# RWKV-7 recurrence into a two-level MoE on one core: the next chunk's transpose ahead of the last one's, and heads placed by pair parity

## The chip, the cores and the metric

The kernel runs on one core of a Trainium2 chip. The metric is the device time of one execution in microseconds (us). TensorE (PE) does the matrix products, VectorE (DVE) and ScalarE (ACT) work on rows of 128 partitions, GpSimd (POOL) does elementwise work more slowly, and SyncE (SP) issues DMAs. Each engine takes its instructions in the order written in the program, apart from what semaphores make it wait for. PSUM has eight banks, into which TensorE writes.

## The reference

Everything is float32. First a recurrence per batch and head (4 batches, 8 heads, 768 steps, head size 40), then a mixture of experts on its output:

```python
for t in range(S):
    y[:, :, t] = np.einsum('bhd,bhde->bhe', rt, state)
    Sa = np.einsum('bhde,bhe->bhd', state, at)
    state = state * wt[:, :, None, :] - np.einsum('bhd,bhe->bhde', Sa, bt) \
            + np.einsum('bhd,bhe->bhde', vt, kt)
x = y.transpose(0, 2, 1, 3).reshape(3072, 320)
# per token: best of 4 groups (softmax of x @ w_group), best of its 4 experts,
# out = g_w * e_w * relu(x @ w1[g, e]) @ w2[g, e]
```

## The kernel before

The recurrence is done in 6 chunks (c) of 128 steps, each in two halves (c2) of 64. The 32 heads form two streams z of two batches each; a stream has 8 pairs i of heads, and j = 0, 1 is the head within a pair. `each()` runs over the 16 heads of a stream. A "half chunk" below is one pass q = 2c + c2 of the main loop, for both streams (c0 and c1).

For a chunk, all steps within a half are solved at once by a triangular inverse. `prep` makes the decay factors with two scans (`back`, `forth`) and multiplies them into `At` (`mul_a`) and the k and b keys (`mul_kb`). `products` (L426) makes the head's 64x64 products: the masked part `g` into G (VectorE, L433), the triangular part `t` into TT (ScalarE, L438, L439) and the transposed keys into KN (L453). Only the 32x32 diagonal blocks of the triangle are solved step by step: VectorE turns them (`solve_load`, L465), GpSimd masks and copies them (L469, L476) and takes 30 steps of two operations each (L486, L488); VectorE turns the result back twice (`turn_x`, L495, into X1; `turn_d`, L499, into DT). The off-diagonal block follows by two products, `merge_a` (L514, copied by L519) and `merge_b` (L528, copied by L531), with `move_d` (L505) moving a block in between; these are the joins. There are two of each per chunk, one for each half.

The chain of a half chunk and a stream is: `right` (L550 with G and v, L552 with At and the state, added in PSUM; copied to RHS by L554), `turn` (the state transposed, L559, into Sn), `ut` (L574, copied into VT by L577), `u` (L566, copied into VN), `update` of the state (L584, L586, and L589 at a chunk's end), `m` (L595, masked into MN by VectorE, L599), `y_state` (L605) and `y` (L612, scaled into R by L614). `finish` (L621) transposes y of the chunk before and makes the gate's logits; `finish_out` copies them (`xn`, L629) and reduces (L630).

The order is written by hand (the tile framework's manual schedule): each engine's queue is in the order of the calls in the loop over q. In the loop of chunk c, `products` and `prep` work for chunk c+2, so that GpSimd solves chunk c+1 or c+2 while the chain of c runs. PSUM's eight banks are three rings: four "nar" (products, m, finish), two "one" (ut, y_state, joins) and two "seq" (right, turn, u, update). After the last chunk comes the MoE, from 407 us on. Arrays lie with head j of a pair on partitions 64j to 64j+39.

## Time and profile before

| | |
|---|---|
| median of 3 runs | 705.15 us (704.52 to 708.0) |
| profiled execution | 709.33 us, span 707.6 us |
| PE matmul, busy | 601.4 us (85%), 11852 records |
| PE weight load | 513.3 us (73%) |
| DVE | 367.5 us (52%), 651 |
| ACT | 277.2 us (39%), 726 |
| POOL | 295.3 us (42%), 428 |
| granted clock, mean | 0.936 of full speed |

The profiled execution is one run; its span leaves out 1.73 us around it. Busy shares are means over two different parts: the recurrence until about 417 us, with all engines at work, and the MoE, with TensorE alone nearly full. A float32 matmul call shows as two records. "[0.53 <-X]" behind a row is the idle time of its engine just before it, and what ended it; "issue" there means that the profile shows nothing that was waited for. A time "t0" is the start of the first `right` of a half chunk.

### The profile page before, as it was taken

Reading aid. Unit: us, or ns where it says so; the run is one execution under the profiler, and the core shown is the slowest. Engines: PE = TensorE matmul, PEld = TensorE weight load, DVE = VectorE, ACT = ScalarE, POOL = GpSimd, SP = SyncE. Lnnn points to the kernel's source line nnn. Section 1 sums busy time; section 2 is a strip of 40 time slices with the busy share of each in tenths; the row PEclk is TensorE's granted clock in tenths of the full one; section 3 lists DMA queues with packets and bytes.
Section 4 is the critical chain, followed back from the end, with each engine's and each line's share of the span. In section 5 each row is a group of like instructions: output and inputs, shape, how many; then the busy total and the mean of one; then the engine's idle time right before and its main releaser. Section 6 shows DMA issues by size and latency. Waiting matters only on the chain. (4 is left out here: it accounts for less than half of the span.)

```text
span 707.6 us, 26969 instructions
## 1 busy us (share of the span) xinstructions
PE 601.4 (85%) x11852; PEld 513.3 (73%) x11852; DVE 367.5 (52%) x651; ACT 277.2 (39%) x726; POOL 295.3 (42%) x428
## 2 busy tenths in 40 slices
...
GB/s 141 121 114 1 94 27 111 59 69 151 96 86 138 94 47 154 42 185 91 29 50 224 34 58 132 173 251 178 181 183 191 190 194 192 181 177 203 89 13 15
DMA packets 128913, 84.19 MB, mean 119 GB/s; under 512 B 77897, under 2 KB 120967, under 8 KB 128788
## 3 DMA queue, kind: packets, MB, share of 16 engines
...
## 5 line engine op out<-in xcount | busy, mean ns | idle before, releaser
L486 POOL TENSOR_TENSOR tmp<-home,TT 128x30 f32<-128x30 f32 (+9 forms) x150 | 103.5, 690 | 11.4
L488 POOL TENSOR_TENSOR home<-home,tmp 128x30 f32<-128x30 f32 (+9 forms) x150 | 100.9, 672 | 11.8
L854 POOL DMA_INDIRECT out_dram<-homek,dst_v x28 | 27.7, 990 | 170.7 <-DVE homek L853 156.6
L426 PE MATMUL nar<-home,home 64*128 64x128 f32 x768 | 67.9, 317 | 31.5 <-DVE home L394 14.8
L426 PEld LDWEIGHTS nar<-home,home 64*128 64x128 f32 x768 | 58.6, 219 | 37.4 <-issue 20.9
L821 PE MATMUL nar<-homeg,home 128*128 128x192 f32 (+7 forms) x472 | 84.5, 333 | 1.2 <-DVE homeg L806 1.2
L821 PEld LDWEIGHTS nar<-homeg,home 128*128 128x128 f32 x472 | 76.9, 195 | 7.8 <-issue 4.7
L550 PE MATMUL seq<-VN,homeg 64*64 64x40 f32 x768 | 51.8, 238 | 14.5 <-ACT RHS L554 9.7
L438 ACT COPY TT<-nar 32x256 f32<-32x256 f32 x96 | 34.7, 362 | 71.3 <-PE nar L426 36.4
L550 PEld LDWEIGHTS seq<-VN,homeg 64*64 64x64 f32 x768 | 45.1, 143 | 17.4 <-ACT RHS L554 11.0
L552 PE MATMUL seq<-ST,home 64*64 64x40 f32 x768 | 51.1, 236 | 0.0
L599 DVE TENSOR_TENSOR MN<-nar,up 128x512 f32<-128x512 f32 x48 | 30.9, 686 | 37.4 <-PE nar L595 37.3
L842 PE MATMUL one<-home,homeq 128*128 128x320 f32 (+5 forms) x192 | 49.5, 436 | 0.0
L433 DVE TENSOR_TENSOR homeg<-nar,up 64x256 f32<-64x256 f32 x80 | 33.4, 418 | 23.9 <-ACT TT L439 16.0
L552 PEld LDWEIGHTS seq<-ST,home 64*64 64x64 f32 x768 | 45.2, 146 | 0.0
L469 POOL TENSOR_SCALAR_AFFINE_SELECT TT<-TT 128x1024 f32<-128x1024 f32 x6 | 8.3, 1379 | 83.1 <-DVE TT L465 83.1
L842 PEld LDWEIGHTS one<-home,homeq 128*128 128x128 f32 (+5 forms) x192 | 30.3, 172 | 16.1 <-issue 1.1
L842 PE MATMUL one<-home,DT 128*128 128x320 f32 (+4 forms) x160 | 40.6, 435 | 0.0
L831 ACT ACTIVATE homeq<-nar 128x384 f32<-128x384 f32 (+5 forms) x14 | 7.3, 524 | 80.9 <-PE nar L829 55.0
L792 POOL DMA_INDIRECT homeq<-x_nat,src_i x4 | 4.6, 1151 | 82.2 <-DVE pad L651 63.8
L853 DVE TENSOR_SCALAR homek<-one,homek 128x320 f32<-128x320 f32 (+4 forms) x15 | 8.2, 550 | 57.9 <-PE one L842 57.9
L595 PE MATMUL nar<-home 64*64 64x64 f32 x1536 | 31.7, 221 | 5.9 <-issue 5.7
...
## 6 DMA issues: line engine op xcount, KB each, us to landing
...
```

Of the source, the lines that this page charges most:

```text
L426: nc.tensor.matmul(ps[j][:, i, :], lhsT=KB[half(j), i0 + i, c2], rhs=At[half(j), 0:b + 1:b, :], start=True, stop=True)
L433: nc.vector.tensor_tensor(G[half(j), hs], ps[j][half(j), :, HW:], up2[half(j), None, :].broadcast_to([HW, NH, HW]), op=ALU.mult)
L438: nc.scalar.copy(out=TT[q:q + HB, ns], in_=ps[j][q:q + HB, :, HW:])
L486: eng.tensor_tensor(t3, W[:, r0:r2, s:s + 1].broadcast_to([P, m, n]), sub[:, s:s + 1, s + 1:].broadcast_to([P, m, n]), op=ALU.mult)
L488: eng.tensor_tensor(W[:, r0:r2, s + 1:], W[:, r0:r2, s + 1:], t3, op=ALU.subtract)
L550: nc.tensor.matmul(ps[half(1 - j), i, :], lhsT=self.G[half(j), i, :], rhs=self.VN[half(j), i, j, :], start=True, stop=False)
L552: nc.tensor.matmul(ps[half(1 - j), i, :], lhsT=self.At[half(j), 1 + 2 * i + self.c2, :], rhs=S0[half(j), i, :], start=False, stop=True)
L595: nc.tensor.matmul(ps[j][half(h), i, :], lhsT=self.VT[half(j), i, h, :], rhs=self.R[half(j), i, self.ts], start=True, stop=True)
L599: nc.vector.tensor_tensor(self.MN[:, j], ps[j], up2[:, None, :].broadcast_to([P, NI, HW]), op=ALU.mult)
L821: nc.tensor.matmul(ps[:, f, :], lhsT=w1s[:, ko, (g0 + f) * P:(g0 + f + 1) * P], rhs=xT[:, ko, :], start=(f == 0 and ko == 0), stop=False, ...
L842: nc.tensor.matmul(ps[half(k % 2, n)] if two else ps[:n], lhsT=hts[e % 2][:, f, h * P:h * P + n], rhs=wbuf[e % 3][2][:, f, :], start=(k < ...
L854: nc.gpsimd.indirect_dma_start(out=out[:, :], out_offset=bass.IndirectOffsetOnAxis(ap=part_of(dst_i, dst_v, n, h, e), axis=0), in_=yt[:n], ...
```

## The change

What the diff does:

- At, R, VT, VN and DT are laid out so that the head of a pair sits by parity. In At the two heads of a pair lie in different columns, each on its own 64 partitions, and the other 64 partitions of these columns take G (`g` writes there). VN holds v on one half and the state on the other (`put_state`, ScalarE copies after the states are updated). So `right` is one product of 128 rows where there were two of 64 added in PSUM.
- `mul_a` in one piece for 128 columns per head parity is `mul_at`; the mask `mask_g` works on 64 partitions at a time; `scale` is copied by ScalarE.
- R and VT hold even and odd pairs on different partitions (`load_two`), and `ut`, `m`, `y_state`, `y` use rows and columns accordingly; `ut` and `y_state` take both "one" banks.
- `turn` turns two heads with one product and writes a "one" bank.
- The joins are one product for two heads; results are copied in four quarters per join. X1 is gone, its place is the right part of the DT that is not in use.
- `solve_mask` writes W itself, and the copy is gone. `solve(c + 2)` stands ahead of `turn_x(c + 1)`. The guard sums W instead of the masked block, and later.
- In even half chunks, the four `finish` stand together ahead of both first joins, and the last joins follow; in odd ones both `right` and `turn` stand ahead of the products of the other chunk, one half of which moves behind `u`. `y_state` moves behind `update` and behind the second `products`, and the last half of `products` ahead of the last `y`.
- The tail's scratch tiles move from `homeg` to the end of `home1`; the guard's bound takes account of the diagonal.

```diff
+        def put_state(c, c2, z):
+            for j in range(2):
+                nc.scalar.copy(out=state["vn", c, c2, z][half(j), :, j, :], in_=ST[z][c2][half(j)])
+
...
-                nc.vector.tensor_copy(out=scale, in_=Rr[:, :, 1])
+                nc.scalar.copy(out=scale, in_=Rr[:, :, 1])
...
+            def mul_at():
+                for j in range(2):
+                    mine = At[half(j), 1:, :].rearrange("p (i k e) t -> p i k (e t)", k=2, e=2)[:, :, j, :]
+                    nc.vector.tensor_tensor(mine, mine, pq[half(j), :, :L], op=ALU.mult)
...
             def g(j):
+                o = half(1 - j)
+                dst = At[o, of_head(j, c2, i0, NH), :]
                 if raw:
...
         def mask_g(c, c2, z):
-            G = state["g", c, c2, z][0]
-            nc.vector.tensor_tensor(G, G, up2[:, None, :].broadcast_to([P, NI, HW]), op=ALU.mult)
+            for j in range(2):
+                o = half(1 - j)
+                mine = state["p", c, z][0][o, of_head(j, c2), :]
+                nc.vector.tensor_tensor(mine, mine, up2[o, None, :].broadcast_to([HW, NI, HW]), op=ALU.mult)
...
-        def solve_mask(c):
-            sub = state[c][:, :, :HB]
-            nc.gpsimd.affine_select(out=sub, in_=sub, compare_op=ALU.is_ge, fill=0.0, base=-1,
+        def solve_start(c, eng):
+            W, sub = ws[c % 2], state[c][:, 0]
+            state["W", c], state["sub", c] = W, sub
+            nc.gpsimd.affine_select(out=W, in_=sub, compare_op=ALU.is_ge, fill=0.0, base=-1,
                                     pattern=[[-1, HB], [1, HB]], channel_multiplier=0)
-            state["sub", c] = sub
-
...
         def guard(c):
-            nc.vector.tensor_reduce(out=t_sum[:, c, :], in_=state["sub", c], axis=AX.X, op=ALU.add,
+            nc.vector.tensor_reduce(out=t_sum[:, c, :], in_=state["W", c], axis=AX.X, op=ALU.add,
...
         def merge_a(c, c2):
-            TT = state[c]
-            ps = bank([P, NS, NI, HB], "one")
-            for z in range(NS):
-                for i, j in each():
-                    q, o = j * HW, j * HW + HB
-                    n = (c2 * NS + z) * NI + i
-                    nc.tensor.matmul(ps[o:o + HB, z, i, :], lhsT=TT[q:q + HB, n, HB:],
-                                     rhs=X1[q:q + HB, n, :], start=True, stop=True)
-            PX = X1[:, c2 * NS * NI:(c2 + 1) * NS * NI, :]
+            TT, X1 = state[c], x1(c)
+            n0, nn = c2 * NS * NI, NS * NI
+            ps = bank([P, nn // 2, HW], "one")
+            for k in range(nn // 2):
+                for j in range(2):
+                    rows, ns = half(j, HB), slice(n0 + 2 * k, n0 + 2 * k + 2)
+                    nc.tensor.matmul(ps[half(j), k, :], lhsT=TT[rows, 1, ns, :], rhs=X1[rows, ns, :], start=True, stop=True)
             for j in range(2):
                 o = j * HW + HB
-                nc.scalar.copy(out=PX[o:o + HB], in_=ps[o:o + HB].rearrange("p z i t -> p (z i) t"))
+                for e in range(2):
+                    nc.scalar.copy(out=TT[o:o + HB, 1, n0 + e:n0 + nn:2, :],
+                                   in_=ps[j * HW + e * HB:j * HW + (e + 1) * HB, :, e * HB:(e + 1) * HB])
...
             for j in range(2):
-                nc.scalar.copy(out=DT[half(j, HB), c2 * NS * NI:(c2 + 1) * NS * NI, HB:],
-                               in_=ps[half(j, HB)])
+                for e in range(2):
+                    nc.scalar.copy(out=DT[half(j, HB), n0 + e:n0 + nn:2, HB:],
+                                   in_=ps[j * HW + e * HB:j * HW + (e + 1) * HB, :, e * HB:(e + 1) * HB])
...
             def right(self):
-                S0 = self.S0
                 ps = bank([P, NI, D], "seq")
                 for i, j in each():
-                    nc.tensor.matmul(ps[half(1 - j), i, :], lhsT=self.G[half(j), i, :], rhs=self.VN[half(j), i, j, :],
-                                     start=True, stop=False)
-                    nc.tensor.matmul(ps[half(1 - j), i, :], lhsT=self.At[half(j), 1 + 2 * i + self.c2, :],
-                                     rhs=S0[half(j), i, :], start=False, stop=True)
+                    nc.tensor.matmul(ps[half(j), i, :], lhsT=self.At[:, 1 + 4 * i + 2 * j + self.c2, :],
+                                     rhs=self.VN[:, i, j, :], start=True, stop=True)
                 nc.scalar.copy(out=self.RHS, in_=ps)
 
             def turn(self):
-                ps = bank([P, NI, D], "seq")
-                for i, j in each():
-                    nc.tensor.matmul(ps[half(j, D), i, :], lhsT=self.S0[half(j), i, :], rhs=eye[half(j), :D],
+                ps = bank([P, NI, D], "one")
+                for i in range(NI):
+                    i0 = i - i % 2
+                    nc.tensor.matmul(ps[half(i % 2, D), i0:i0 + 2, :], lhsT=self.S0[:, i, :], rhs=wsel[:, 0, :2 * D],
                                      start=True, stop=True)
                 nc.scalar.copy(out=self.Sn[:, :, :D], in_=ps)
...
             def ut(self):
-                ps = bank([P, NI, HW], "one")
+                ps = [bank([P, NI // 2, HW], "one") for _ in range(2)]
                 for i, j in each():
-                    nc.tensor.matmul(ps[half(j, D), i, :], lhsT=self.RHS[half(1 - j), i, :],
-                                     rhs=self.DT[half(1 - j), self.un * NI + i, :], start=True, stop=True)
+                    nc.tensor.matmul(ps[j][half(i % 2, D), i // 2, :], lhsT=self.RHS[half(j), i, :],
+                                     rhs=self.DT[half(j), self.un * NI + i, :], start=True, stop=True)
                 for j in range(2):
-                    nc.scalar.copy(out=self.VT[half(j), :, 1 - j, :], in_=ps[half(j)])
+                    nc.scalar.copy(out=self.VT[:, j::2, 1, :], in_=ps[j])
...
                 for i, j in each():
+                    k, n = i % 2, i - i % 2 + j
                     for h in range(2):
-                        nc.tensor.matmul(ps[j][half(h), i, :], lhsT=self.VT[half(j), i, h, :],
-                                         rhs=self.R[half(j), i, self.ts], start=True, stop=True)
+                        nc.tensor.matmul(ps[k][half(1 - j if h == 0 else j), n, :], lhsT=self.VT[half(k), n, h, :],
+                                         rhs=self.R[half(k), n, self.ts], start=True, stop=True)
...
             def y_state(self):
-                self.ps_y = bank([P, NI, HW], "one")
+                self.ps_y = [bank([P, NI // 2, HW], "one") for _ in range(2)]
...
+                for k in range(2):
+                    nc.vector.tensor_tensor(self.R[:, k::2, self.ts], self.ps_y[k], self.pq[:, k::2, self.ts], op=ALU.mult)
...
+        ALL2 = (("back",), ("mul_kb", 0), ("forth",), ("mul_at",), ("mul_kb", 1))
...
-                pre(("back",))
+                finish(c - 1, 1, 0)
+                finish(c - 1, 1, 1)
+                merge_a(c, 0)
                 merge_a(c, 1)
-                move_d(c, 1)
-                if q == 2 * NC - 4:
-                    choose(0, N3, fl, rl, (1,))
-                finish(c - 1, 1, 0)
-                merge_b(c, 0)
-                finish(c - 1, 1, 1)
                 finish_out(c - 1, 1, 0)
                 finish_out(c - 1, 1, 1)
                 load_r(c, 1)
-                merge_b(c, 1)
+                pre(("back",))
+                if q == 2 * NC - 4:
+                    choose(0, N3, fl, rl, (1,))
+                for c2_ in range(2):
+                    move_d(c, c2_)
+                    merge_b(c, c2_)
                 if q == 2 * NC - 4:
                     rank_products(0, N3)
                     ranks(0, N3)
                     seen_by(N3)
-                pre(("forth",), ("mul_kb", 0), ("mul_a", 0))
+                pre(("forth",), ("mul_kb", 0), ("mul_at",))
...
+                c0.right()
+                if q >= 2 * NC - 3:
+                    choose(*new_gate[q], fl, rl, (0,))
+                c0.turn()
+                if new:
+                    load_at(*new)
+                pre(("back",))
+                c1.right()
+                c1.turn()
+                if old:
+                    products(*old, 1, 0)
+                pre(("forth",))
                 if q >= 2 * NC - 3:
                     choose(*new_gate[q], fl, rl, (1,))
-                pre(("mul_kb", 0), ("mul_a", 0))
             c0.ut()
             c0.u()
+            if c2:
+                if old:
+                    products(*old, 1, 1)
+                pre(("mul_kb", 0), ("mul_at",))
...
-            c0.y_state()
             c0.m()
             c0.update()
+            c0.y_state()
...
                     load_vn(*nxt, z)
+                for z in range(NS):
+                    put_state(*nxt, z)
...
-            c1.y_state()
             c1.m()
             if nxt:
                 for z in range(NS):
                     load_vt(*nxt, z)
-            if q:
-                pre(("mul_a", 1))
             if new:
                 products(*new, 0, 1)
+            c1.y_state()
...
+            kn1 = products(*new, 1, 1, late=True) if kn else None
             c1.y()
             if kn is not None:
                 kn()
+                kn1()
                 pre(("squares", 0))
             if q == 0:
                 pre(("mul_kb", 1), ("mul_a", 1))
-                guard(1)
-            elif c2 == 0 and c + 1 < NC:
-                guard(c + 1)
-            if c2 and new:
-                products(*new, 1, 1)
-            if c2 and c + 1 < NC:
+            if c2 == 0:
+                guard(c)
+            elif c + 1 < NC:
+                if new:
+                    solve(c + 2, PO)
                 turn_x(c + 1)
-                if new:
-                    solve_load(c + 2)
-                    solve_mask(c + 2)
-                    solve_start(c + 2, PO)
-                    solve_steps(c + 2, PO, 0, HB)
                 turn_d(c + 1)
```

ScalarE's queue in an even half chunk (chunk 2), from the copies behind the first `right` on; `one_109` and `one_110` are the two "one" banks, `home_116` is VT, `DT` the inverse. Before:

```order
L519 COPY X_134<-one_109 32x512 x2
L505 COPY DT_121<-DT_121 32x16x32 x2
L629 COPY xn<-nar_105 128x320
L629 COPY xn<-nar_106 128x320
L519 COPY X_134<-one_110 32x512 x2
L505 COPY DT_121<-DT_121 32x16x32 x2
L531 COPY DT_121<-one_109 32x16x32 x2
L629 COPY xn<-nar_107 128x320
L629 COPY xn<-nar_108 128x320
L531 COPY DT_121<-one_110 32x16x32 x2
L577 COPY home_116<-one_109 64x8x64 x2
```

Now:

```order
L651 COPY xn<-nar_106 128x320
L539 COPY TT<-one_109 32x8x32 x4
L539 COPY TT<-one_110 32x8x32 x4
L651 COPY xn<-nar_107 128x320
L651 COPY xn<-nar_108 128x320
L526 COPY DT_120<-DT_120 32x16x32 x2
L553 COPY DT_120<-one_109 32x8x32 x4
L526 COPY DT_120<-DT_120 32x16x32 x2
L553 COPY DT_120<-one_110 32x8x32 x4
L406 COPY scale<-Rr 128x8
L597 COPY home_116<-one_109 128x4x64
L597 COPY home_116<-one_110 128x4x64
```

The copies of the two first joins (L539) now stand together behind the first two `xn` (one is shown), all four `xn` stand ahead of the moves (L526), and `ut`'s copies (L597) take both banks.

VectorE's queue in an odd half chunk, from the `back` scan to MN of the first stream; `homeg` is G, `home_115` At of the chunk ahead, `nar` the banks of `products` and of `m`. Before:

```order
L383 SCALAR_TENSOR_TENSOR Rr<-home_114,first 128x1040
L385 RECIPROCAL first<-Rr 128x8
L433 TENSOR_TENSOR homeg<-nar_105,up_132 64x256
L433 TENSOR_TENSOR homeg<-nar_106,up_132 64x256
L388 SCALAR_TENSOR_TENSOR homeq<-home_114,first 128x1040
L390 COPY scale<-Rr 128x8
L433 TENSOR_TENSOR homeg<-nar_107,up_132 64x256
L433 TENSOR_TENSOR homeg<-nar_108,up_132 64x256
L398 TENSOR_TENSOR home_114<-home_114,Rr 128x8x128
L394 TENSOR_TENSOR home_115<-home_115,homeq 128x8x64
L599 TENSOR_TENSOR MN<-nar_105,up_132 128x512
```

Now, with MN (L620) next:

```order
L399 SCALAR_TENSOR_TENSOR Rr<-home_114,first 128x1040
L401 RECIPROCAL first<-Rr 128x8
L457 TENSOR_TENSOR home_116<-nar_105,up_131 64x4x64
L457 TENSOR_TENSOR home_116<-nar_106,up_131 64x4x64
L404 SCALAR_TENSOR_TENSOR homeq<-home_114,first 128x1040
L457 TENSOR_TENSOR home_116<-nar_107,up_131 64x4x64
L457 TENSOR_TENSOR home_116<-nar_108,up_131 64x4x64
L421 TENSOR_TENSOR home_114<-home_114,Rr 128x8x128
L417 TENSOR_TENSOR home_115<-home_115,homeq 64x8x128 x2
L620 TENSOR_TENSOR MN<-nar_105,up_131 128x512
```

The copy of `scale` has left the queue, and At's multiply is two pieces that cover both halves of the chunk; one multiply by the window (L421) stands ahead of it as before.

The end of VectorE's queue in an odd half chunk, where the solved blocks are turned. Before:

```order
L614 TENSOR_TENSOR home_116<-one_110,homeq 128x8x64
L433 TENSOR_TENSOR homeg<-nar_107,up_132 64x256
L433 TENSOR_TENSOR homeg<-nar_108,up_132 64x256
L495 STREAM_TRANSPOSE X_134<-home_115 128x32x32
L465 STREAM_TRANSPOSE TT<-TT 128x32x32
L499 STREAM_TRANSPOSE DT_121<-home_115 128x32x32
```

Now:

```order
L636 TENSOR_TENSOR home_116<-one_109,homeq 128x4x64
L636 TENSOR_TENSOR home_116<-one_110,homeq 128x4x64
L491 STREAM_TRANSPOSE TT<-TT 128x32x32
L516 STREAM_TRANSPOSE DT_121<-home_115 128x32x32
L520 STREAM_TRANSPOSE DT_120<-home_115 128x32x32
```

The turn of the next triangle (L491), on which GpSimd waits, now stands ahead of the turn of the solved one (L516), which waits for GpSimd; the last masks of `products` stand ahead of the last multiply of y.

## Rows read from the trace of the kernel before

**Rows 1.** Busy time by stretch: length, PE, PEld, DVE, ACT, POOL, clock, DMA share, GB/s.

```profile
92.87:144.29 51.42, 42.24 (x1384) 39.57 (x1376) 40.33 (x54) 32.09 (x88) 46.64 (x63) 0.93 0.28 61
137.89:197.20 59.31, 52.04 (x1730) 47.92 (x1729) 43.71 (x59) 37.15 (x99) 49.78 (x73) 0.97 0.44 103
197.20:227.83 30.63, 26.70 (x994) 24.56 (x992) 21.64 (x28) 19.85 (x47) 23.46 (x35) 1.00 0.45 111
227.83:252.34 24.51, 23.34 (x739) 21.60 (x737) 21.43 (x31) 16.57 (x50) 22.25 (x29) 1.00 0.40 85
252.34:308.20 55.86, 49.64 (x1731) 46.20 (x1729) 43.46 (x59) 36.74 (x97) 46.08 (x65) 1.00 0.40 96
...
407.00:707.60 300.60, 281.11 (x1758) 215.65 (x1750) 69.11 (x177) 33.57 (x107) 63.51 (x64) 0.98 0.47 153
146.59:150.00 3.41, 3.41 (x82) 3.35 (x76) 3.41 (x2) 1.16 (x2) 1.65 (x2) 0.50 0.02 5
```

**Rows 2.** GpSimd's line of time around the end of a solve.

```profile
253.44 0.27 POOL L488 TENSOR_TENSOR home<-home,tmp 128x30 f32<-128x30 f32 x1
258.64 1.27 POOL L469 TENSOR_SCALAR_AFFINE_SELECT TT<-TT 128x1024 f32<-128x1024 f32 x1 [4.94 <-DVE TT L465]
```

**Rows 3.** TensorE's line of time in the even half chunk from 197.20.

```profile
197.20 0.32 PE L550 MATMUL seq<-VN,homeg 64*64 64x40 f32 x4
...
198.74 0.31 PE L552 MATMUL seq<-ST,home 64*64 64x40 f32 x4
...
202.65 1.20 PE L514 MATMUL one<-X,TT 32*32 32x32 f32 x64
203.78 1.83 PE L621 MATMUL nar<-wsel,home 128*64 128x100 f32 x32
...
212.69 0.70 PE L574 MATMUL one<-DT,RHS 64*40 64x64 f32 x18 [1.42 <-issue]
...
217.06 0.27 PE L595 MATMUL nar<-home 64*64 64x64 f32 x1
217.10 0.23 PE L605 MATMUL one<-home,Sn 64*64 64x64 f32 x2
217.16 1.10 PE L595 MATMUL nar<-home 64*64 64x64 f32 x62
...
220.32 0.69 PE L584 MATMUL seq<-VN,homek 128*40 128x40 f32 x25 [1.17 <-issue]
220.81 1.10 PE L612 MATMUL one<-MN,homek 128*40 128x64 f32 x32
```

**Rows 4.** ScalarE's line of time in the same half chunk, the joins.

```profile
203.90 1.17 ACT L519 COPY X<-one 32x512 f32<-32x512 f32 x2 [0.70 <-PE one L514]
205.09 1.26 ACT L505 COPY DT<-DT 32x512 f32<-32x512 f32 x2
206.37 0.75 ACT L629 COPY xn<-nar 128x320 f32<-128x320 f32 x2
...
211.46 1.17 ACT L531 COPY DT<-one 32x512 f32<-32x512 f32 x2
```

**Rows 5.** VectorE's line of time in the odd half chunk from 227.83.

```profile
237.01 1.55 DVE L398 TENSOR_TENSOR home<-home,Rr 128x1024 f32<-128x1024 f32 x1
238.48 1.08 DVE L394 TENSOR_TENSOR home<-home,homeq 128x512 f32<-128x512 f32 x1
241.07 1.29 DVE L599 TENSOR_TENSOR MN<-nar,up 128x512 f32<-128x512 f32 x2 [1.51 <-PE nar L595]
...
254.58 1.95 DVE L495 STREAM_TRANSPOSE X<-home 128x1024 f32<-128x1024 f32 x1
```

**Rows 6.** Groups of instructions: count, busy us, mean ns, idle time before.

```profile
L438 ACT COPY TT<-nar 32x256 f32<-32x256 f32 x96 | 34.7, 362 | 71.3 <-PE nar L426 36.4 <-DVE homeg L433 14.4 <-POOL tmp L486 9.6
...
L461 DVE TENSOR_TENSOR homeg<-homeg,up 128x512 f32<-128x512 f32 x4 | 4.6, 1195 | 0.0
```

**Rows 7.** TensorE's line of time, the first join of the half chunk from 137.89.

```profile
146.26 1.72 PE L514 MATMUL one<-X,TT 32*32 32x32 f32 x64 [2.53 <-DVE X L495]
```

143 lines of the change are left out of this document (67 added, 76 removed).

## The prediction

> **What bounds the kernel now.** I read the table of stretches first [rows 1]. The tail from 407.00 on is 300.60 us with TensorE busy 281.11 of them; the diff moves two scratch tiles there and nothing else, so I take it as unchanged. All gain or loss lies in the first 407 us. A steady chunk of 128 tokens is an even and an odd half chunk, counted from the first product of `right` to the next one: 30.63 and 24.51. TensorE is busy 26.70 and 23.34 of them, VectorE 21.64 and 21.43, GpSimd 23.46 and 22.25. TensorE is nearest to full, so the plain reading is that it is the bound. The second view is GpSimd's line of time [rows 2]: the solve of one chunk ends at 253.71 and the next starts at 258.64, after 4.94 of waiting for VectorE's transpose. VectorE comes to the transpose that reads a solve's result at 254.58, without a wait [rows 5]. So GpSimd is not the bound either, though it is within a microsecond of being it, and its own work per chunk is 55.1 less that gap, 50.2, and less still by the copy that goes. The third view is TensorE's line of time through one even half chunk [rows 3]. Ahead of `ut` there is a gap of 1.42 that the profile calls issue; ScalarE's last join copy ends at 212.63, beside the end of that gap [rows 4]. In the odd half chunk VectorE waits 1.51 for `m` before MN at 241.07 [rows 5]. Three engines are close to each other, and each works in order.
>
> **TensorE's part.** `right` goes from 64 records of two quadrants to 32 over all 128 rows. The old groups of four take 1.54 for 52 records [rows 3], 29.6 ns each and 1.87 in all; `y`, which has the new shape, does 32 in 1.10. I take 1.03: 0.83 less per chain. `turn` goes from 32 records to 16 twice as wide: nothing. `ut` and `y_state` go from two quadrants to four: `m` does 62 records in four in 1.10, 18 ns each, so 32 take about 0.57 where at 29.6 they take 0.95: 0.37 less each. A join goes from 64 records in 1.20 to 32, about 0.93 by the same pace; with one first or last join per chain that is 0.27 at most, and I take 0.15. Sum 1.7 per chain, less what `m` may lose: its calls now stand four in a row on one row half, where the half changed after two. I put it at 1.35 instead of 1.10. Net 1.45 per chain, four chains per chunk: 5.8 of 50.0. If TensorE were alone, each chunk would gain that.
>
> The rows show that matmuls of neighbours do change places: a record of `m` starts at 217.06, ahead of records of `y_state` at 217.10, all of which stand before it in the order [rows 3]. The Trainium skill, page "TensorE: Matmul & The Clock Gate", Part 3 on packing small matmuls, has them in strict program order, with no reordering. The row speaks against it here; by that rule `m` would only ever pair two quadrants in the new order, which is rival C.
>
> **Even half chunk.** `right`, `turn`, `right`, `turn` now stand in a row (2 x 1.03 and 2 x 0.67: 3.4), then all four `finish` products (3.64, by 1.83 for two), then both first joins. The first one ends at t0+8.0, where it ended at t0+6.65 (202.65 and 1.20). From there ScalarE's queue is in order. A join's result is now copied in four quarters, as the two heads of a pair come from different places: 0.365 each by the row of the 32x256 copy [rows 6], 1.46 where two copies took 1.17 [rows 4]. So: four, four, two `xn` (0.75), two moves (1.26), four, two moves, four: 4 x 1.46 + 0.75 + 2 x 1.26 = 9.1, ending at t0+17.1. Before, `ut` of the first chain waited for the first bank of the joins alone. It now writes two banks, and the second is the one that the last join's copies empty. So `ut` starts at t0+17.2; it went on after its gap at t0+15.5. TensorE has nothing from t0+12 to t0+17.2. From 212.69 to the next half chunk it took 15.14; less 1.2 of an issue gap at 220.32, less 0.37 for two `ut` and two `y_state` each (1.48), 0.5 more for `m`, and 0.2 for the records ahead of 212.69, that is 13.2. Even half chunk: 17.2 + 13.2 = 30.4. Issue gaps may come back, 0 to 1.5; I take 0.7 and put it in the sum.
>
> **The clock.** After 2.53 without TensorE work before 146.26 the granted clock was 0.50 (1.2 GHz) from 146.59 to 150.00, and the join there took 1.72 where it takes 1.20 [rows 1, 7]. The hole of 5 us would do the same to `ut`, `u` and `m` behind it. Half of 3.4 us is 1.7 of work; I take 1.3 on the path, with bounds 0 and 1.7.
>
> **Odd half chunk.** VectorE has two scans, four masks, the multiply by the window (1.55) and one of At (1.08) ahead of MN, and without the wait it was ready at t0+11.7 [rows 5]. At now holds two heads apart, on 64 partitions each, and is multiplied as two pieces of 64x1024: between 2 x 1.08, the row of 512 elements, and 2 x 1.55, the row of 1024 beside GpSimd; 2.7 taken. VectorE is ready at t0+13.4. TensorE has `m` done at t0+10, since one half of `products` stands behind `ut` and `u` now; it waits, and its gain is lost in VectorE's queue. From MN on it took 11.3 to the next half chunk. The last `y` now stands behind the last half of `products`, whose banks come free only when VectorE's masks and ScalarE's copies of an earlier half are done: 0.8 more, 12.1. Sum 25.5, bounds 24.0 and 26.5.
>
> **What costs nothing here.** GpSimd's solve loses its copy and its gap, 6 us of GpSimd's time, and none of the end while the other engines need 55; the cover is theirs, and GpSimd is what is next when they shrink. The four copies of states into VN per half chunk fall into ScalarE's idle time, 30.63 less 19.85. Twelve more DMA issues per chunk stand on SP's queue with nothing that is waited for at once behind them. The guard reads W one half chunk later at the same cost.
>
> **Start.** Up to 144 VectorE carries most (40.33 of the last 51.42 [rows 1]). Added: eight-head masks, four of 64 partitions for two of 128, +2.4 by 1.195 each [rows 6], twice; and the multiply of At in four preparations, about +1.0 each. Part of this is covered by idle time, so of some 9 us I take 6 at t=137.9; bounds 3 and 9.
>
> **End.** In the last four half chunks the solves and then the products end, so TensorE carries a larger part still than the 23.34 of 24.51 of the odd half chunk [rows 1], and its saving counts. Even -1 and 0, as the copies' hole stays; odd -4.4 and -3.0, as there is no preparation ahead of MN and 2.9 to 3.2 of TensorE's work goes. -8.4.
>
> **Sum.** Start +6. Pairs of half chunks, even 30.4 + 1.3 and odd 25.5: 57.2 against 55.14 from 197.20 (+2.1) and 55.86 from 252.34 (+1.3) [rows 1]. The pair from 137.89 took 59.31, with the wait of 2.53; GpSimd starts earlier now, the wait goes, and I put it at 57.7 (-1.6). End -8.4. Returning issue gaps 4 x 0.7 = +2.8. Total +2.2: no change beyond what shows. The profiled run was 709.33 for a span of 707.60, so it would become 711.5; the median of the runs shown is 705.15, 4.2 below the profiled one, and the same difference on it gives **707**. This case's own range is 699 to 714.
>
> **Rivals.**
> *A, TensorE was the bound and the gain is paid out.* A chunk falls to GpSimd's 49.5 to 50: -6 for three chunks, -8.4 at the end, +6 at the start: 705 - 20 = 685. For it: TensorE's 23.34 of 24.51. Against: the queues of ScalarE and VectorE worked out above.
> *B, slower.* The holes of 2.6 in odd half chunks lower the clock too, as the 2.53 before 146.26 did: 1.3 more in each of five, with the start at +9 and the end at -6. That is 6.5 + 3 + 2.4 on top of the forecast, 719. It decides once TensorE's hole in odd half chunks is as long as that one.
> *C, matmuls keep their order.* `m` then costs 1.87 instead of 1.10, and not the 1.35 taken: 0.52 more in each of 24 chains, 18 of them on the path (in six the wait for VectorE hides it): +9.4, 716. This is what the rule of the Trainium skill named above would make of the change; that page stands alone against the row.
> *D, the solves don't close up,* as the last copies into TT hold back the transpose ahead of GpSimd. The forecast stays; A then stops at -10, 695.
>
> **Chances.** Forecast 0.50: of it faster 0.11, same 0.27, slower 0.12. A with its part of D 0.26, faster. B 0.16 and C 0.08, slower. Faster by over 0.5% 0.37, within 0.5% (3.5 us, about what a measurement of this kernel can tell from no change) 0.27, slower 0.36. The range goes from A to just short of B: 685 to 718.
>
> **What would show it.** Right: in even half chunks `ut` first at t0+17, with TensorE idle ahead of it and the granted clock lower behind it; in odd ones VectorE at MN without a wait, TensorE waiting for MN; GpSimd's solves at most 1 us apart and done well ahead of the transpose that reads them; the half chunk of 137.9 some 6 later. Wrong: chunks of 50 with GpSimd never idle and the transpose waiting for it (A); `m` in 1.9 (C); `ut` at t0+14 (the two banks then are not the wait).

## The result and the profile after

The changed kernel takes 713.73 us (median of 20 runs, 708.84 to 717.42); the kernel before takes 707.14 in the 20 runs made beside them. The ratio is 1.011, with an interval of 1.0087 to 1.0134: about 7 us slower. The forecast of 707 stood on a base of 705.15. The measured time lies in its range of 685 to 718, and just inside the narrower 699 to 714, but what was forecast was no change, and the change is a loss.

The traces compared are of one execution each: 709.33 us before (span 707.60) and 713.00 after (span 710.90). That is a difference of 3.3 in the spans, less than the 6.6 between the medians, because the profiled run of before was 2.2 above its median and that of after 0.7 below. What follows places the 3.3; where the rest lies in the other runs the two traces can't show.

The first lines of the page after: the span, then busy time, share of the span and records of each engine.

```profile
span 710.9 us, 23391 instructions
...
PE 581.1 (82%) x9932; PEld 491.8 (69%) x9932; DVE 384.0 (54%) x670; ACT 300.0 (42%) x836; POOL 299.7 (42%) x421
```

TensorE has 20 us less to do than before (601.4) in 1,920 records fewer. VectorE has 16.5 more and ScalarE 22.8 more. The mean granted clock fell from 0.936 to 0.889.

Busy time by stretch after, with the columns of [rows 1]. The first row ends where half chunk q = 2 starts, the next five are q = 2 and 3 together, 4, 5, and 6 and 7 together, then the last four half chunks, then the tail.

```profile
0.00:150.03 150.03, 83.34 (x1601) 75.44 (x1602) 122.64 (x181) 99.46 (x268) 63.79 (x109) 0.73 0.35 78
150.03:206.13 56.10, 46.74 (x1416) 43.29 (x1413) 45.88 (x61) 40.23 (x115) 46.86 (x63) 0.88 0.46 109
206.13:236.87 30.74, 25.37 (x775) 23.68 (x772) 23.77 (x29) 22.83 (x62) 25.05 (x35) 0.83 0.43 105
236.87:262.75 25.88, 21.66 (x647) 19.76 (x645) 22.00 (x31) 16.95 (x53) 21.79 (x28) 0.93 0.40 85
262.75:320.42 57.67, 47.33 (x1414) 43.69 (x1412) 45.64 (x60) 40.13 (x114) 46.78 (x62) 0.88 0.40 98
320.42:420.32 99.90, 83.40 (x2595) 77.45 (x2590) 60.60 (x149) 47.54 (x123) 32.26 (x63) 0.88 0.34 93
420.32:710.90 290.58, 273.22 (x1523) 208.54 (x1520) 63.51 (x163) 32.83 (x105) 63.19 (x64) 0.98 0.48 157
```

The same view of the kernel before, from q = 2 to the end of q = 7:

```profile
137.89:308.20 170.31, 151.72 (x5187) 140.27 (x5185) 130.24 (x175) 110.30 (x290) 141.57 (x201) 0.99 0.42 100
```

| stretch | before | after | difference | forecast |
|---|---|---|---|---|
| start, up to q = 2 | 137.89 | 150.03 | +12.14 | +6 |
| q = 2 to 7 | 170.31 | 170.39 | +0.1 | +1.8, and issue gaps +2.8 in all |
| q = 8 to 11 | 108.70 | 99.90 | -8.8 | -8.4 |
| tail | 290.70 | 290.58 | -0.1 | 0 |

So the steady part is where it was although TensorE's work there fell from 151.72 to about 141.1 (the four rows of after), the end pays out as forecast, and the start costs twice what was put on it.

**An even half chunk.** TensorE's line of time in the half chunk from 206.13 (start, busy, operation, records, and the idle time ahead with what ended it):

```profile
206.13 1.08 PE L571 MATMUL seq<-VN,home 128*64 128x40 f32 x32
...
209.06 2.92 PE L643 MATMUL nar<-wsel,home 128*64 128x100 f32 x64
211.91 2.08 PE L535 MATMUL one<-DT,TT 32*64 32x64 f32 x64
214.64 3.48 PE L549 MATMUL one<-DT,TT 32*64 32x64 f32 x64 [0.66 <-ACT TT L539]
219.58 0.43 PE L594 MATMUL one<-DT,RHS 64*40 64x64 f32 x2 [1.46 <-ACT DT L553]
222.38 0.98 PE L594 MATMUL one<-DT,RHS 64*40 64x64 f32 x27 [2.36 <-ACT DT L553]
```

`ut` (L594) starts at t0+13.46, with the first of its two banks, does two records and stops. The other 30 wait 2.36 us for the second bank and start at t0+16.25. Both waits name L553, the last joins' copies, which are the end of this queue on ScalarE:

```profile
213.10 3.00 ACT L539 COPY TT<-one 32x256 f32<-32x256 f32 x8 [2.02 <-PE one L535]
...
218.04 1.49 ACT L553 COPY DT<-one 32x256 f32<-32x256 f32 x4
...
220.84 1.49 ACT L553 COPY DT<-one 32x256 f32<-32x256 f32 x4
```

From 213.10 to 222.33 are 9.23 us without an idle stretch; the forecast added up 9.1 for the same queue, ending at t0+17.1 where it ended at t0+16.2.

**The clock.** Two stretches of the same half chunk (the granted clock stands third from the end of each row):

```profile
211.91:215.50 3.59, 2.94 (x94) 2.80 (x94) 1.16 (x3) 2.31 (x7) 2.96 (x9) 0.99 0.46 142
215.50:225.50 10.00, 6.04 (x136) 5.44 (x135) 8.73 (x8) 7.78 (x20) 9.45 (x8) 0.50 0.63 165
```

Of the two levels, 2.4 and 1.2 GHz, TensorE runs at the lower for 10 us. The fall comes at 215.50, while the last joins run. That is 0.9 after a hole of 0.66 ahead of these joins, and 2.6 before the first of the holes in front of `ut` opens, at 218.12. The same half chunk before was at 1.00 throughout [rows 1].

**An odd half chunk.** VectorE's line of time in the one that starts at 236.87:

```profile
246.61 3.15 DVE L417 TENSOR_TENSOR home<-home,homeq 64x1024 f32<-64x1024 f32 x2
249.79 1.29 DVE L620 TENSOR_TENSOR MN<-nar,up 128x512 f32<-128x512 f32 x2
```

VectorE comes to MN (L620) at t0+12.9 without a wait, and the wait of 1.51 in [rows 5] is gone: `m` had been done since t0+9.7.

### The profile page after: what moved, and what is told of

It is laid out like the page before. It is cut to its first block, busy times and chain, and to the rows that moved or that the text cites. A ratio compares the mean times of both kernels' runs of the same rounds, so it can differ in the third digit from the quotient of the medians.

```text
span 710.9 us, 23391 instructions
## 1 busy us (share of the span) xinstructions
PE 581.1 (82%) x9932; PEld 491.8 (69%) x9932; DVE 384.0 (54%) x670; ACT 300.0 (42%) x836; POOL 299.7 (42%) x421
## 5 line engine op out<-in xcount | busy, mean ns | idle before, releaser
L509 POOL TENSOR_TENSOR home<-home,tmp 128x30 f32<-128x30 f32 (+9 forms) x150 | 110.5, 737 | 11.8
L843 PE MATMUL nar<-home,home 128*128 128x192 f32 (+7 forms) x320 | 57.3, 331 | 1.2 <-DVE home L828 1.2
L843 PEld LDWEIGHTS nar<-home,home 128*128 128x128 f32 x320 | 51.9, 190 | 6.2 <-issue 3.5
L457 DVE TENSOR_TENSOR home<-nar,up 64x256 f32<-64x256 f32 x80 | 33.8, 422 | 29.3 <-PE nar L448 14.7
L594 PE MATMUL one<-DT,RHS 64*40 64x64 f32 x768 | 26.8, 266 | 24.1 <-ACT DT L553 20.1
L620 DVE TENSOR_TENSOR MN<-nar,up 128x512 f32<-128x512 f32 x48 | 30.8, 682 | 25.6 <-PE nar L616 25.5
L496 POOL TENSOR_SCALAR_AFFINE_SELECT home<-TT 128x1024 f32<-128x1024 f32 x6 | 8.6, 1435 | 82.0 <-DVE TT L491 82.0
L594 PEld LDWEIGHTS one<-DT,RHS 64*40 64x40 f32 x768 | 20.2, 143 | 29.1 <-ACT DT L553 22.7
L586 PE MATMUL seq<-RHS,DT 64*64 64x40 f32 x768 | 36.8, 257 | 0.0
L853 ACT ACTIVATE DT<-nar 128x384 f32<-128x384 f32 (+5 forms) x12 | 6.3, 527 | 70.3 <-PE nar L851 55.5
L633 PE MATMUL one<-MN,homek 128*40 128x64 f32 x768 | 28.8, 225 | 8.7 <-DVE MN L620 7.9
```

The costliest lines, as they stand in the source:

```text
L457: nc.vector.tensor_tensor(dst, ps[j][o, :, HW:], up2[o, None, :].broadcast_to([HW, NH, HW]), op=ALU.mult)
L509: eng.tensor_tensor(W[:, r0:r2, s + 1:], W[:, r0:r2, s + 1:], t3, op=ALU.subtract)
L586: nc.tensor.matmul(ps[half(j), i, :], lhsT=self.DT[half(j), self.un * NI + i, :], rhs=self.RHS[half(j), i, :], start=True, stop=True)
L594: nc.tensor.matmul(ps[j][half(i % 2, D), i // 2, :], lhsT=self.RHS[half(j), i, :], rhs=self.DT[half(j), self.un * NI + i, :], start=True, ...
L620: nc.vector.tensor_tensor(self.MN[:, j], ps[j], up2[:, None, :].broadcast_to([P, NI, HW]), op=ALU.mult)
L633: nc.tensor.matmul(self.ps_y[k][half(j, D), i // 2, :], lhsT=self.KN[:, j, i, :], rhs=self.MN[:, k, n, :], start=False, stop=True, skip_gr ...
```

## The experiments

All ratios are to the kernel before, in runs made beside it; the changed kernel stands at 1.011. Profiled runs lie up to 5.2 us from the median of their kernel, so lengths of single half chunks are compared, and whole times by their ratios. Lengths of the changed kernel for comparison: even half chunks q = 2, 4, 6 took 31.29, 30.74 and 31.77 (before 33.02, 30.63, 31.56), odd ones 24.81, 25.88 and 25.91 (before 26.29, 24.51, 24.30).

### The bank that `ut` waits for: e1_bseq

The last joins take a "seq" bank, so that `ut`'s second bank doesn't wait for their copies.

```diff
         def merge_b(c, c2):
...
-            ps = bank([P, nn // 2, HW], "one")
+            ps = bank([P, nn // 2, HW], "seq")
```

> The changed kernel with one thing different: the last joins write seq banks, so that the two banks of `ut` are those of the first joins, empty since long. Changed kernel: 713.7, even half chunk 30.7 to 31.8, first record of `ut` at t0+13.5 and the second bank only at t0+16.3. Theory, the two banks are the wait: `ut` goes through at t0+13.5; but its copies still stand behind those of the last joins in ScalarE's queue, so 1.0 to 1.5 per even half chunk and 1.2 in the first one, 706 to 708. If the bank alone were the whole delay, 2.4 each, 702. Rival, the joins' copies in ScalarE's queue are all that counts and the bank nothing: 713.

Measured 708.13, ratio 0.999 (0.9964 to 1.0017). TensorE's line of time in the half chunk that starts at 200.64:

```profile
209.17 1.15 PE L549 MATMUL seq<-DT,TT 32*64 32x64 f32 x32 [0.44 <-ACT TT L539]
210.69 1.97 PE L549 MATMUL seq<-DT,TT 32*64 32x64 f32 x30 [0.38 <-ACT TT L539]
212.99 0.43 PE L594 MATMUL one<-DT,RHS 64*40 64x64 f32 x2 [0.33 <-ACT DT L553]
213.77 1.35 PE L594 MATMUL one<-DT,RHS 64*40 64x64 f32 x29 [0.34 <-ACT DT L553]
```

`ut` goes on at t0+13.1 instead of t0+16.25, with no hole over 0.44 ahead of it. One word of the diff gives back the whole loss: the two ratios are 1.2% apart and their intervals don't overlap. But the even half chunks came to 30.35, 31.31 and 30.41, only 0.6 shorter on average. More shows in q = 0 (80.52 instead of 84.08), at q = 8 (29.38 instead of 31.56) and q = 10 (33.61 instead of 34.58). Together that is 1.7 + 3.6 + 2.2 + 1.0 = 8.5, about the 1.2%, and most of the 10.1 by which the two spans differ (700.8 for 710.9; the profiled run of e1 was 5.2 below its median). So the time came near the expected 706 to 708, but from other parts: 1.0 to 1.5 was expected in each even half chunk and 1.2 in the first one. And the clock falls all the same:

```profile
200.64:208.00 7.36, 7.36 (x221) 7.24 (x217) 6.93 (x8) 5.00 (x16) 3.62 (x10) 1.00 0.16 51
208.00:225.00 17.00, 14.83 (x367) 13.45 (x365) 11.74 (x11) 13.52 (x34) 15.67 (x18) 0.60 0.45 118
```

`ut` takes 1.35 for 29 records, where at full clock in an odd half chunk 32 take 0.66. So the hole ahead of `ut` isn't what lowers the clock: without it TensorE still spends 13.5 us at the low level, from 210.5 on, within the joins.

### The order of the joins: e2_order

The calls of the even half chunk in the order of before, with the changed joins.

```diff
+                merge_a(c, 0)
+                move_d(c, 0)
...
+                pre(("back",))
+                merge_a(c, 1)
+                move_d(c, 1)
...
+                merge_b(c, 0)
...
-                merge_a(c, 0)
-                merge_a(c, 1)
...
-                for c2_ in range(2):
-                    move_d(c, c2_)
-                    merge_b(c, c2_)
+                merge_b(c, 1)
```

> The changed kernel with the order of before in even half chunks: first join, move, two `finish`, second first join, move, and last joins between the other two `finish`. Theory (the copies in quarters, not the order, make the length): ScalarE starts 3 earlier, at t0+6, but has one `xn` pair more and the same 9 to 10 us ahead of `ut`; `ut` at t0+15.5 to 16.5, 711 to 714. Rival, the order with all `finish` first is what costs: `ut` at t0+13.5 to 14, 2.5 less in five half chunks, 701.

Measured 710.25, ratio 1.0049 (1.0011 to 1.0088). The steady even half chunks don't gain (31.23, 32.08, 31.93): `ut` still stops 2.05 for its second bank, and a new hole of 1.88 stands at t0+3.1, where the first join now waits for VectorE's turn (L516) of the solved blocks. The gain is at the end, q = 8 with 29.05 and q = 10 with 32.31, for 31.56 and 34.58. The second bank comes at t0+16.8, a little later than the 15.5 to 16.5 of the theory, and the rival's 701 is out. By the medians the order gives back half of what the bank does, but its interval all but touches that of e1 on one side and that of the changed kernel on the other.

### The clock: e4_unused and e4b_unused

Products whose result nobody reads stand behind the first and the last joins, so that TensorE isn't idle there. e4 does so in all even half chunks from q = 2 on, with 4 and 24 of them; e4b only while there is a chunk c+2, with 4 and 20.

```diff
+        def unused(n):
+            t = banks["nar"][0]
+            for _ in range(n):
+                nc.tensor.matmul(t[:, :P], lhsT=ones, rhs=up, start=True, stop=True)
...
+                if new:
+                    unused(4)
                 for c2_ in range(2):
                     move_d(c, c2_)
                     merge_b(c, c2_)
+                if new:
+                    unused(20)
```

> The changed kernel with products that nobody uses in the hole of TensorE in even half chunks (4 ahead of the last joins, 24 behind them, 128x128 by 128, into a free bank). Theory, the low clock behind the joins costs time on the path: granted clock 1.00 where it was 0.50 from t0+9.5 to t0+19.5, `ut`, `u` and `m` 1.5 to 2.5 shorter, five half chunks: 702 to 706. Rival, the clock is low where TensorE isn't on the path: 713 to 715.

e4 measured 721.77, ratio 1.0175 (1.013 to 1.022): a miss by 16. Its q = 2, 4, 6 are 0.6 shorter on average at a clock of 1.00, but q = 8 took 36.47 and q = 10 39.05, 4.9 and 4.5 more, as the unused products there stood in the way of work that was ready.

> As e4_unused, with 4 and 20 unused products and only in half chunks 2, 4 and 6, where the first one was 0.6 shorter each with `ut` 0.4 late from the products themselves; it lost its time in half chunks 8 and 10, where they stood in the way. Theory, the low clock costs about 1 on the path per even half chunk: 30.0 to 30.3 each, 710 to 712. Rival, it costs nothing: 31.3 as in the changed kernel, 713 to 715.

e4b measured 711.92, ratio 1.0113 (1.0062 to 1.0165): as a whole it can't be told from the changed kernel. Its windows can. The 10 us that were at 0.50 are now:

```profile
213.00:223.00 10.00, 9.82 (x237) 9.34 (x239) 8.40 (x7) 8.92 (x24) 9.37 (x9) 1.00 0.61 160
```

and the three even half chunks took 29.91, 29.89 and 30.31, 1.2 less on average. `ut`'s second bank comes at t0+16.26 there, as in the changed kernel (16.25), so what is gained lies behind it and is the price of the low clock; the forecast had put 1.3 on it. Three times 1.2 is half a per cent, less than e4b's interval is wide, so the whole time doesn't show it.

### VectorE ahead of MN: e6_no_mul_at

At's multiply is left out of the preparations in the loop.

```diff
-                pre(("forth",), ("mul_kb", 0), ("mul_at",))
+                pre(("forth",), ("mul_kb", 0))
...
-                pre(("mul_kb", 0), ("mul_at",))
+                pre(("mul_kb", 0))
```

> The changed kernel without the multiply of At in the preparations of chunks 2 to 5 inside the loop (seven of them); the output is wrong then, its time is that of VectorE without 3.1 in each half chunk. Theory: in odd half chunks MN waits for VectorE, so MN of the first stream at t0+10 instead of t0+12.9 and half chunks 3, 5 and 7 shorter by 2.5 to 3; even ones 0 to 0.5: 704 to 707. Rival (VectorE has slack there, the copies of ScalarE hold it): 711 to 714.

Measured 704.95, ratio 0.9985 (0.9946 to 1.0024). MN of the odd half chunk that starts at 235.10 begins at t0+9.7:

```profile
244.75 1.27 DVE L620 TENSOR_TENSOR MN<-nar,up 128x512 f32<-128x512 f32 x2
```

The odd half chunks take 22.61, 22.66 and 23.07: 2.2 to 3.2 less, the 3.15 of the two pieces. The even ones stay (31.49, 31.96, 31.96). VectorE holds the odd half chunks and doesn't hold the even ones, and 704 to 707 was expected on that ground.

### The last copies into TT and GpSimd: e3_turn_first

`turn_x(c + 1)` back ahead of `solve(c + 2)`, as before.

```diff
+                turn_x(c + 1)
                 if new:
                     solve(c + 2, PO)
-                turn_x(c + 1)
```

> The changed kernel with the turn of the solved blocks again ahead of the load of the next triangle. The pauses between GpSimd's solves in the changed kernel are 2.9, 4.8, 5.5 and 6.2. Theory (the pause is what a chunk takes beyond a solve; the order of the two turns does not set it): pauses 2 longer, no half chunk longer by over 0.5, 712 to 715. Rival (solves unbroken are worth something): 2 more per chunk, 719 to 722.

Measured 714.13, ratio 1.012 (1.0077 to 1.0163), the same as without it. GpSimd's pauses are 4.65, 4.6, 6.4 and 5.2, where the changed kernel has 2.9, 4.8, 5.5 and 6.2. GpSimd's line of time at the end of a solve of the changed kernel:

```profile
260.51 0.26 POOL L509 TENSOR_TENSOR home<-home,tmp 128x30 f32<-128x30 f32 x1
266.24 1.27 POOL L496 TENSOR_SCALAR_AFFINE_SELECT home<-TT 128x1024 f32<-128x1024 f32 x1 [5.46 <-DVE TT L491]
```

It is the wait of [rows 2], 0.5 longer. A solve lasts 51.4 and a chunk 56.6 (206.13 to 262.75); the pause is what is left. The new order of the turn decides nothing: put back, it makes the pauses 0.4 longer on average, where 2 was expected, and the time no worse. e3 moves the turn and not the copies into TT. On these the trace of the changed kernel speaks: the last one (L463) ends at 263.66, and VectorE begins the turn (L491) at 264.04 without a wait, straight from the last masks and a multiply of y; two of these masks had waited 0.3 and 0.4 for such copies. That the pause is set by the length of the chunk is a reading of these times; no run shortens the chunk to 51.

### Joins out of the way: e7_late and e8_back_early

e7 puts only the first half's joins ahead of `ut`; the second half's stand behind the second stream's `u`, in "nar" banks. e8 moreover puts the `back` scan right behind the turns, the gate's reductions behind the scans and the guard into the odd half chunk.

```diff
+            late = q and not c2
+            if late:
+                merge_a(c, 1, "nar")
+                move_d(c, 1)
...
+            if late:
+                merge_b(c, 1, "nar")
+            if q:
+                pre(("squares", 1))
```

> The changed kernel with the joins of the second half (needed only in the odd half chunk) moved behind `u` of the second stream, into nar banks, and the first joins started at t0+5 right behind `turn`. Theory, ScalarE's queue of joins ahead of `ut` is what holds the even half chunk: `ut` at t0+11 without a gap, even half chunks 4 to 5 shorter, until GpSimd's 51.5 per chunk binds: 694 to 700. Rival, the moved joins only move the wait (to `m` and the products that wait for their banks): 706 to 712.

e7 measured 705.53, ratio 0.9971 (0.9934 to 1.0009), where 694 to 700 was expected and 706 to 712 by the rival. `ut` starts at t0+12.2 and `m` is done at t0+18.0 to t0+19.4, but the half chunks are 30.32, 29.97 and 31.05. VectorE comes to MN only at t0+21.4. Its scans stood behind the gate's reduction (L652), which waited 3.17 for a copy of ScalarE's:

```profile
217.48 0.57 DVE L652 TENSOR_REDUCE lg<-nar 128x20 f32<-128x80 f32 x2 [3.17 <-ACT xn L651]
...
229.12 1.29 DVE L620 TENSOR_TENSOR MN<-nar,up 128x512 f32<-128x512 f32 x2
```

> e7_late, whose `m` was done at t0+18.5 while MN waited for VectorE until t0+21.4 (VectorE stood 3.2 idle behind the turns, with the back scan queued behind the gate's reduce that waits for ScalarE), with the back scan right behind the turns, the reduces behind the scans, and the guard in the odd half chunk behind MN of the second stream. Theory, VectorE's queue took up what the joins gave back: MN at t0+18.5 to 19, even half chunks 27 to 28, odd ones 24 to 25 by the guard: 692 to 698, GpSimd's pauses then 0 to 1.5. Rival, the next engine (ScalarE) holds it: 702 to 706.

e8 measured 704.94, ratio 0.9972 (0.9935 to 1.0009). VectorE now waits for `m` instead:

```profile
228.44 1.29 DVE L620 TENSOR_TENSOR MN<-nar,up 128x512 f32<-128x512 f32 x2 [1.53 <-PE nar L616]
```

and the half chunks are 30.50, 31.89 and 30.39, no shorter. Two waits were taken away in turn and the half chunk stayed at 30 to 32; e7's theory was missed by 5.5 us and e8's by 6.9, and e8's rival, 702 to 706 with another engine as the next to hold, has the time. TensorE's line of time in e8 shows a first join that waits 2.06 for the turn (1.87 in e7), and `finish` behind it at a lower clock:

```profile
213.31 1.15 PE L535 MATMUL one<-DT,TT 32*64 32x64 f32 x32 [2.06 <-DVE DT L516]
214.38 4.62 PE L643 MATMUL nar<-wsel,home 128*64 128x100 f32 x64
```

Those 64 records take 2.92 in the changed kernel. What e8 gains, it gains at the end: q = 8 starts 1.0 later than in the changed kernel, but q = 8 takes 28.72 for 31.56 and q = 10 28.39 for 34.58.

### The start: e5_masks_pool and e9_start

e5 gives the start's masks of G to GpSimd, which has nothing to do there. e9 adds the "seq" bank for the last joins of q = 0, and GpSimd for one multiply of At.

```diff
-                nc.vector.tensor_tensor(mine, mine, up2[o, None, :].broadcast_to([HW, NI, HW]), op=ALU.mult)
+                nc.gpsimd.tensor_tensor(mine, mine, up2[o, None, :].broadcast_to([HW, NI, HW]), op=ALU.mult)
```

> The changed kernel with the masks of the first stream's G, eight pieces of 64x512 ahead of the loop and in half chunk 0, on GpSimd, which is idle there. Theory, the start's 12 us are VectorE's queue and what the low clock adds behind it: 1.9 less ahead of the first solve (the other half of the masks ran beside GpSimd's select there) and up to 3.7 in half chunk 0: third half chunk's start (t0 of q2, 150.0) 4 to 5.6 earlier, 708 to 710. Rival, TensorE at half clock and ScalarE's copies hold half chunk 0, not VectorE: 0 to 2 earlier, 712 to 714.

e5 measured 714.95, ratio 1.0114 (1.0062 to 1.0166): nothing gained, q = 2 at 150.83. GpSimd's masks and VectorE's first solve met. One row of GpSimd, then VectorE's beside it:

```profile
37.46 5.30 POOL L487 TENSOR_TENSOR home<-home,up 64x512 f32<-64x512 f32 x4
```

```profile
41.52 1.34 DVE L507 TENSOR_TENSOR tmp<-home,TT 128x84 f32<-128x84 f32 x1
42.89 0.25 DVE L509 TENSOR_TENSOR home<-home,tmp 128x84 f32<-128x84 f32 x1
```

In q = 0, without the masks on VectorE, its scan waits for ScalarE's squares (L425) instead:

```profile
102.92 2.33 DVE L399 TENSOR_TENSOR_SCAN Rr<-home,first 128x1040 f32<-128x1040 f32 x1 [3.64 <-ACT junk L425]
```

> e5_masks_pool with two more edits of the start alone: the last joins of half chunk 0 into seq banks (e1_bseq had half chunk 0 at 80.5 instead of 84.1), and At of the second chunk's first stream multiplied by GpSimd (2.5 less for VectorE). Theory: the third half chunk starts 8 to 11 earlier than in the changed kernel, near the kernel before (137.9), and everything behind it as in the changed kernel: 702 to 705. Rival: the gains overlap, 4 to 6: 708.

e9 measured 711.98, ratio 1.0072 (1.0046 to 1.0098), with q = 2 at 150.96: a miss by 7 us or more.

### All together: e10_all and e11_best

e10 is e8 with e9's start, and two `finish` ahead of the first join; e11 is e10 without GpSimd's part at the start, so that of the start's edits only the "seq" bank in q = 0 remains.

```diff
-                merge_b(0, 0)
+                merge_b(0, 0, "seq")
```

> e8_back_early with the start of e9_start, and with two `finish` ahead of the first join, so that TensorE has work while it waits for the turn (e8 stood 2 us there and had the clock at 0.50 for `finish` behind it). Theory: 8 to 10 from the start, and 0.5 to 1 per even half chunk from the hole: 693 to 697, faster than both. Rival: the two halves of gain overlap in GpSimd's solve (51.5 per chunk and 2 to 4 for the turns), chunks stay at 55 to 56: 698 to 701.

e10 measured 704.91, ratio 0.9959 (0.9927 to 0.9991), where 693 to 697 or 698 to 701 was expected. Its interval ends just under 1: some 0.4% faster than the kernel before, if that.

> e10_all without GpSimd's help at the start (masks and the multiply of At are VectorE's again; with them VectorE's first solve steps took 1.3 where they take 0.25, and the start was 1.5 later), keeping the last joins of half chunk 0 in seq banks. Theory: half chunk 0 as in e1_bseq (80.5, third half chunk at 145 to 146.5 instead of 150.5), the rest as in e10_all: 699 to 701, about 1% faster than the kernel before. Rival: the start's gain is taken up by the wait for GpSimd's second solve, 703 to 705.

e11 measured 703.57, ratio 0.9971 (0.9943 to 1.0). It is 1.4% better than the changed kernel, by the two ratios, and not to be told from the kernel before, nor from e10. The 699 to 701 was missed; the time is in the rival's 703 to 705, though in the traces the start's gain isn't taken up (q = 8 starts at 313.18, in e10 at 321.02). In the traces q = 2 starts at 144.31 in e11 and at 150.51 in e10, but the two times are 1.3 apart, and e11's profiled run, at 700.5, was 3.1 below its median and e10's, at 706.89, 2.0 above. So no price for the start is taken from this pair.

In e11 a middle even half chunk is still 32.07 long, though `ut` starts at t0+10.1. From 210 to 227.4 its clock is 0.61:

```profile
210.00:227.40 17.40, 15.44 (x386) 14.58 (x386) 10.35 (x14) 12.29 (x33) 15.75 (x22) 0.61 0.56 145
```

The records there, with TensorE full, are slow ones:

```profile
214.75 1.90 PE L586 MATMUL seq<-RHS,DT 64*64 64x40 f32 x30
216.58 1.97 PE L535 MATMUL nar<-DT,TT 32*64 32x64 f32 x32
218.47 2.04 PE L616 MATMUL nar<-home 64*64 64x64 f32 x64
```

In its odd half chunks, at full clock, 32 records of `u` (L586) take 1.09 and `m` 1.23; a join of this half chunk ahead of the fall takes 1.15. So these three rows, 5.91 together, hold about 2.5 of slowness (0.8 to 0.9 each). What an earlier `ut` saved was paid out again, for a part at least, at the low clock. Whether e11 with its clock kept up would be the faster kernel was not tried, and the other parts of the 30 us stay open.

## Why the prediction was right, and where it wasn't

**`ut` and its second bank: right.** It was put at t0+17.2, and its second bank came at t0+16.25. Its parts hold too: ScalarE's queue took 9.23 for 9.1, and e1 shows that the bank is the reason. The two records that start at t0+13.46 are the first product, whose bank is free; they meet the sign named for a wrong step, `ut` at t0+14, in the letter, but all that follows waits for the second bank. Even half chunks were put at 31.7 and came to 31.3 on average; the 0.7 set aside for each pair's returning issue gaps was not needed. What the forecast did not see is what the wait is worth: e1, which takes it away, is as fast as the kernel before.

**The clock: size right, cause wrong.** 1.3 per even half chunk was taken, and e4b shows 1.2. But it was drawn from [rows 1] as half of 3.4 us behind a hole. The low stretch lasts 10 us; it begins in the joins, and e1 keeps it without the hole. Most of it cost nothing, as TensorE had work in only 6 of those 10 us and then waited for copies. So the size is right by luck. What makes the clock fall in the joins stays open; e4b shows only that with TensorE kept busy there it doesn't.

**Odd half chunks: the queue right, the sum in part by luck.** 25.5 forecast, 25.53 on average. MN without a wait at t0+12.9 (forecast 13.4); e6 moves it by the price of At's multiply, 3.15 for the 2.7 taken, just over the upper bound of 3.1. From MN on 12.1 was taken and 12.0, 13.0 and 13.1 came, so one term's 0.5 too much makes up for the other's 0.6 too little.

**The odd half chunks' low clock, rival B: half of it came.** The granted clock falls to about half for 3.5 us in each. Ahead of the fall TensorE stands 2.23, not for MN, as B had it, but for a copy of the keys:

```profile
256.59 2.26 PE L448 MATMUL nar<-home,home 64*128 64x128 f32 x16 [2.23 <-ACT homek L477]
```

```profile
256.50:260.00 3.50, 3.41 (x50) 3.08 (x52) 1.55 (x4) 1.29 (x6) 2.87 (x9) 0.53 0.28 57
```

The length of 25.53 has this in it, so the 1.3 that B would have added to 25.5 doesn't show, and B's 719 wasn't reached. A is out in the steady part: TensorE was less busy and the chunks were no shorter. In the odd half chunks e6 shows VectorE's queue to hold them; in the even ones e1, e7 and e8 each took a wait away and left 30 to 32, so what holds these is not shown. A came true only at the end, as the forecast had it too.

**TensorE's part: `m` half right, joins wrong, no matter.** `m` takes 1.22, where 1.35 was taken, so rival C with its 1.87 is out. Records of neighbours still change places:

```profile
244.82 0.27 PE L616 MATMUL nar<-home 64*64 64x64 f32 x1
244.85 0.37 PE L586 MATMUL seq<-RHS,DT 64*64 64x40 f32 x5
```

A record of `m` (L616) starts ahead of five of `u` (L586), which stand ahead of it in the order. The Trainium skill, page "TensorE: Matmul & The Clock Gate", Part 3, has small matmuls in strict program order; this trace disagrees again. `right` is 1.08 (1.03 taken), `ut` 0.66 and `y_state` 0.69 (0.57 taken for each). A join with half the records saves next to nothing: 1.15 in e8, and 2.08 for two in a row, where one took 1.20 and 0.93 was taken. All of this stands beside waits and moves no end, except in the last four half chunks, where the sum of -8.4 came to -8.8. There the odd ones came as forecast, -4.4 and -3.4 for -4.4 and -3.0; the even ones came to +0.7 and -1.8 for -1 and 0, two misses that cancel.

**GpSimd: wrong, and in contradiction with the rest.** Pauses of at most 1 us were named as a sign; they are 2.9 to 6.2. With chunks of 57.2 and solves of 50.2 a pause of 7 follows from the forecast's own numbers. Rival D's copies into TT don't make it: they end 0.4 ahead of the turn, and VectorE comes to the turn without a wait. The solves also got longer, 51.4 for 50.3, though a copy is gone. The consequence for the time, nothing, was right.

**The start: the mis-sized step.** +6 was taken, bounds 3 and 9, and +12.1 came. The times in the two traces divide it in three. The turn of the second triangle (L491) is 5.0 later (95.59 for 90.57); from there to the start of q = 1 it takes 25.83 for 20.60, which is 5.2 more; and q = 1 is 1.9 longer.

The first part is about the forecast's term. The turn of the first solved blocks is 2.8 later, and the mask of eight heads, two calls before and four now, costs 1.4 more each time:

```profile
97.67 3.74 DVE L487 TENSOR_TENSOR home<-home,up 64x512 f32<-64x512 f32 x4
```

(Before it was 2.30 by two calls, at 92.69.) Not all of the 5.0 need be VectorE's: ahead of 90.16 TensorE stands 1.83, and the profile names a load of At there. No run isolates it.

The second part is what the term left out. The forecast had worked out the bank wait for the other even half chunks, and q = 0 is one too. TensorE's line of time in its chain, after:

```profile
104.43 1.97 PE L549 MATMUL one<-DT,TT 32*64 32x64 f32 x32 [3.95 <-ACT home L597]
...
107.99 0.98 PE L594 MATMUL one<-DT,RHS 64*40 64x64 f32 x27 [1.23 <-ACT DT L553]
```

The 3.95 is a bank that `ut`'s copy (L597) has to empty. The kernel before waited for the same copy, and nearly as long:

```profile
97.13 1.61 PE L574 MATMUL one<-DT,RHS 64*40 64x64 f32 x26 [3.64 <-ACT home L577]
```

But there it was the second stream's `ut` itself that waited, where now it is the last join, and `ut` comes only behind that join's copies. e1, where these joins take another bank, needs 22.31 from the turn to q = 1, and so takes 3.5 of the 5.2 away. The copy is also later than it need be: before, it followed ScalarE's squares (L402, L425 now) at once, at 95.91, and now it stands behind the copy of `scale`, which the change had moved there and which waits 2.46 for VectorE's scan:

```profile
103.78 0.20 ACT L406 COPY scale<-Rr 128x8 f32<-128x8 f32 x1 [2.46 <-DVE Rr L399]
104.00 0.65 ACT L597 COPY home<-one 128x256 f32<-128x256 f32 x2
```

That move was listed in the change and priced nowhere. In e5, with the masks gone from VectorE, the copy of `scale` waits 2.39 all the same, since the scan then waits for the squares. The clock is lower too, from 89 to 113 in the changed kernel and then in the kernel before:

```profile
89.00:113.00 24.00, 16.43 (x306) 15.25 (x308) 16.80 (x20) 15.97 (x46) 14.13 (x17) 0.50 0.15 33
```

```profile
89.00:113.00 24.00, 19.87 (x678) 18.81 (x681) 20.32 (x25) 16.21 (x41) 18.36 (x25) 0.86 0.26 57
```

A run isolates one part only, e1's 3.5. What the `scale` copy and the low clock have of the rest, and what makes the 1.9 of q = 1, stays open: no run changes one of them alone.

**The range and the chances.** 685 to 718 held. Slower, which came, had 0.36; of this 0.24 stood on B and C, and C's mechanism did not come and B's in half, so the case that came is nearest to the forecast's own slower end, which had 0.12. In the trace the start is 6.1 over its forecast, and 5.0 of it is offset by the pairs (1.7), the issue gaps (2.8) and the end and tail (0.5), which leaves 3.3 where +2.2 was said. That the errors of the start and of the other parts have opposite signs is luck for the range. Without the start's surplus of 6.1 the two kernels would be within the half per cent that a measurement can tell, which is also where e1 puts them.
